# Spectral gate with a Mish layer: one program part per engine, or all instructions in the main block

## The chip, the cores and the metric

The kernel runs on one core of a Trainium2 chip. The metric is the device time of one execution in microseconds (us). Before the change it is 132.66 us, the median of three runs (132.80, 132.24, 132.66). A core has five engines, each with an instruction stream of its own: PE (matmul, with PEld for its weight loads), ACT, DVE, POOL and SP, which here only issues DMAs and waits. The streams meet only through semaphores: an instruction can wait until a semaphore has reached a value, and can add to one when it is done.

## The reference

```python
x = A_x                                            # 1 x 2048 x 512, bf16
g = sigmoid((x * gate_w).sum(-1, keepdims=True))   # one gate per row
X = rfft2(x.astype(float32), axes=(-2, -1))        # A: a filter in the spectrum
a = irfft2(X * (A_w_r + 1j * A_w_i), s=(2048, 512)).astype(bfloat16)
h = x @ B_w1 + B_b1                                # B: 512 -> 1792
act = h * tanh(softplus(h))                        #    Mish
b = act @ B_w2                                     #    1792 -> 512
return g * a + (1 - g) * b
```

## The kernel before

The 2048 rows are 16 tiles of 128. Branch B is two matmul stages on PE: the first (line 865) forms 14 blocks of 128 hidden columns for each of four chunks of 512 rows, with Mish on ACT (line 870) as it leaves PSUM; the second (line 883) sums 14 products for each row tile. Branch A is done as small matmuls with constant matrices: a transform over the columns (line 622), further ones (637, 716), the filter as DVE products in SBUF (735, 738, 742), and the way back (798, 837), whose results are mixed in by line 891 or by lines 906 and 910. Line 897 (ACT) and line 900 (DVE) scale the sums by 1 - g into the output buffer, which eight DMAs from SP and one from ACT write out (issued at line 485).

The program first gathers all of this as tasks in a graph (`_Graph.add`). `place` goes through a string, ORDER, that names each task in a fixed order, with its engine and its buffers; from it come one list of tasks per engine and the tasks each one waits for. `emit` (line 279) then gives out the instructions. Its inner function `run` (line 293) goes through the list of one engine: it emits the waits (`wait_ge`, line 299), the task's instructions, and the increments. For SP, `run` ends with waits for every DMA semaphore that SP has not waited for yet, the last being `out_sem`, which counts the nine output DMAs:

```python
            if ename == "sp":
                for t in self.tasks:
                    if t.isdma and t.sem is not out_sem:
                        wait(t.sem, t.semval)
                wait(out_sem, 16 * n_out)
```

`run` is called from five small functions inside `with nc.Block() as block:` (line 325). Such a block gives each engine a part of the program of its own. A part begins with a branch from the main block and ends with a branch to a common closing part, in which the five engines meet in a barrier: each one drains (waits until its own instructions are done), adds one to a gather semaphore (96) and waits for a release semaphore (97), which POOL raises when all the others have come. The five functions stand in the order PE, ACT, DVE, POOL, SP.

Ahead of the block, and not part of the change, the object that holds the program writes four small constants with POOL and makes the engines meet in a barrier of the same kind. These rows of the profile stand at line 953, where that object is made.

Of the kernel before, what the change touches and what calls it, by code (L numbers as in the profile page):

```python
# [186 lines left out]
class _Graph:  # L187
# [91 lines left out]
    def emit(self, nc, eng_sem, out_sem, n_out):  # L279
        order = self.order  # L280
        need = set()
        for t in self.tasks:
            for d in t.deps:
                if not d.isdma and not (d.eng == t.eng == "pe"):
                    need.add(id(d))
        for e in ("pe", "act", "dve", "pool"):
            n = 0
            for t in order[e]:
                if id(t) in need:
                    n += 1  # L290
                    t.sig = n

        def run(ename, eobj):
            seen = {}

            def wait(sem_, val):
                if seen.get(sem_.num, 0) < val:
                    seen[sem_.num] = val
                    eobj.wait_ge(sem_, val)

            for t in order[ename]:
                want = {}
                for d in t.deps:
                    if d.isdma:
                        sem_, val = d.sem, d.semval
                    elif d.eng == ename == "pe":
                        continue
                    else:
                        sem_, val = eng_sem[d.eng], d.sig
                    if want.get(sem_.num, (None, 0))[1] < val:  # L310
                        want[sem_.num] = (sem_, val)
                for sem_, val in want.values():
                    wait(sem_, val)
                ins = t.fn(eobj)
                if t.isdma:
                    ins.then_inc(t.sem, 16)
                elif t.sig:
                    ins.then_inc(eng_sem[ename], 1)
# [3 lines that stand above are left out]
                        wait(t.sem, t.semval)  # L322
                wait(out_sem, 16 * n_out)

        with nc.Block() as block:
            @block.tensor
            def _(e):
                run("pe", e)

            @block.scalar  # L330
            def _(e):
                run("act", e)

            @block.vector
            def _(e):
                run("dve", e)

            @block.gpsimd
            def _(e):
                run("pool", e)  # L340

            @block.sync
            def _(e):
                run("sp", e)


ORDER = """
# [620 lines left out]
```

## Time and profile before

| | before |
|---|---|
| median of 3 runs | 132.66 us (132.24 to 132.80) |
| the profiled execution: its own time | 132.7 us |
| its span, from the first to the last of the program's own instructions | 130.6 us |
| what lies around the span | 2.1 us |
| instructions in the trace | 2554 |
| PE busy | 123.9 us (95%) |
| PEld busy | 66.3 us (51%) |
| DVE busy | 92.9 us (71%) |
| ACT busy | 74.0 us (57%) |
| POOL busy | 4.7 us (4%) |
| granted TensorE clock, mean | 0.997 |
| instruction fetches, queue q8 | 8 packets, 0.13 MB |

How to read it: the span is cut by the program's own instructions. Barriers, waits, branches and DMA issues are instructions with rows, but do not count as busy. The trace also holds a record of every change of a semaphore with its time; this record goes on after the span, where the runtime closes the execution with instructions that have no rows here. In the profile, "q" behind an engine's name (SPq) means its sequencer, the part that fetches, waits and issues. L325 is line 325.

### The profile page before, as it was taken

The page shows a single profiled execution, that of the slowest core. Times are in us where ns is not written, and L with a number is a line of the kernel's source. Part 1 is how long each engine was busy: PE and PEld are TensorE (multiplying, and loading weights), DVE is VectorE, ACT ScalarE, POOL GpSimd, SP SyncE. Part 2 cuts the span into 40 slices and gives each one's busy share as a digit, 9 for nine tenths or more (in the row PEclk, how much of TensorE's full clock was granted, in tenths as well). Part 3 has the DMA queues.
Part 4 walks back from the last instruction along what each step waited for, and adds up shares of the span by engine and source line. Part 5 has one row for each costly group of instructions (what it writes and reads, how often), then busy time and mean ns, then how long its engine had stood idle before and what let it go on. Part 6 is the DMA issues. An engine that isn't in the chain of part 4 may idle for free.

```text
span 130.6 us, 2554 instructions
## 1 busy us (share of the span) xinstructions
PE 123.9 (95%) x1058; PEld 66.3 (51%) x1076; DVE 92.9 (71%) x161; ACT 74.0 (57%) x105; POOL 4.7 (4%) x8
## 2 busy tenths in 40 slices
PE   7989999999999999999999999999999999999990
PEld 4844566665654445444454445546654544444440
DVE  0773797999995899999999996237198692712820
ACT  3564989999999879998968024255431520001102
POOL 2000000000470000000000000000000000000000
PEclk9999999999999999999999999999999999999998
DMA  3889998878899989997400002020000002000671
GB/s 104 248 270 366 302 132 280 124 98 112 242 157 139 229 129 318 373 338 257 156 5 0 0 0 55 0 82 0 5 0 0 5 0 80 0 0 0 235 287 40
DMA packets 17302, 16.88 MB, mean 129 GB/s; under 512 B 7628, under 2 KB 14668, under 8 KB 17228
## 3 DMA queue, kind: packets, MB, share of 16 engines
q1 hardware_dynamic: 17120, 16.60, 52.8%
q8 instruction: 8, 0.13, 0.4%
q10 hardware_dynamic: 172, 0.13, 0.3%
q14 instruction: 2, 0.02, 0.1%
HBM read 13.05 MB, written 2.10 MB: 116 GB/s over the span
## 4 chain that ended last, share of the span: by engine, by line
PE 55%; DVE 28%; ACT 5%; DMA 5%; issue 2%; SPq 2%; DVEq 0%
PE ps L883 27%; PE ps L865 14%; DVE rE L742 8%; DVE tmp L735 6%; DMA w_sb<-in_B_w_dram 5%; DVE rC L738 4%; PE ps L837 3%; PE ps L798 3%; PE ps L637 3%; SPq L485 2%; ACT rC L522 2%; DVE rW L667 2%; PE ps L622 2%; DVE rW L679 2%; PE ps L891 1%
## 5 line engine op out<-in xcount | busy, mean ns | idle before, releaser
L865 PE MATMUL ps<-rX,w_sb 128*128 128x512 bf16 x215 | 49.5, 379 | 1.5 <-DMA w_sb<-in_B_w_dram 0.8
L865 PEld LDWEIGHTS ps<-rX,w_sb 128*128 128x128 bf16 x224 | 21.2, 98 | 24.3 <-DMA w_sb<-in_B_w_dram 1.3
L897 ACT ACTIVATE rX<-ps,omg 128x512 bf16<-128x512 f32 x10 | 6.9, 687 | 37.4 <-PE ps L891 22.6
L883 PE MATMUL ps<-w_sb,hs 128*128 128x512 bf16 x107 | 24.2, 379 | 0.6 <-issue 0.3
L870 ACT ACTIVATE hs<-ps,b1f 128x512 bf16<-128x512 f32 x28 | 18.2, 705 | 4.0 <-PE ps L865 2.8
L883 PEld LDWEIGHTS ps<-w_sb,hs 128*128 128x128 bf16 x112 | 10.5, 98 | 11.9
L883 PE MATMUL ps<-w_sb,rD 128*128 128x512 bf16 x54 | 12.5, 379 | 0.2 <-ACT tmp L844 0.2
L883 PE MATMUL ps<-w_sb,rS 128*128 128x512 bf16 x54 | 12.5, 379 | 0.1
L848 DVE TENSOR_TENSOR rA<-tmp,ps 128x512 bf16<-128x512 f32 x16 | 10.0, 680 | 3.4 <-PE ps L837 3.4
L735 DVE TENSOR_TENSOR tmp<-rC,rA 64x1024 bf16<-64x1024 bf16 x16 | 10.8, 685 | 1.9 <-ACT rC L522 1.5
L522 ACT ACTIVATE rC<-ps 128x1024 bf16<-128x1024 f32 x11 | 11.3, 1059 | 1.0 <-PE ps L716 0.6
L604 DVE TENSOR_TENSOR rB<-rA 128x256 bf16<-128x256 bf16 (+1 forms) x14 | 5.8, 458 | 6.5 <-DMA rA<-in_A_x_dram 6.5
L611 DVE SCALAR_TENSOR_TENSOR rA<-rA,tmp 128x512 bf16<-128x512 bf16 x16 | 10.0, 686 | 0.2
L742 DVE TENSOR_TENSOR rE<-rC,tmp 128x1024 bf16<-128x1024 bf16 x8 | 9.8, 1224 | 0.3
L870 ACT ACTIVATE rD<-ps,b1f 128x512 bf16<-128x512 f32 x14 | 9.0, 692 | 0.9 <-PE ps L865 0.9
L870 ACT ACTIVATE rS<-ps,b1f 128x512 bf16<-128x512 f32 x14 | 8.6, 689 | 1.4 <-PE ps L865 1.4
L910 DVE SCALAR_TENSOR_TENSOR rX<-ps,gcol,rX 128x512 bf16<-128x512 f32 x8 | 5.6, 745 | 5.1 <-PE ps L906 5.1
L883 PEld LDWEIGHTS ps<-w_sb,rS 128*128 128x128 bf16 x56 | 5.5, 98 | 6.6
L900 DVE TENSOR_SCALAR rX<-ps,omg 128x512 bf16<-128x512 f32 x6 | 4.5, 747 | 5.8 <-PE ps L891 4.0
L883 PEld LDWEIGHTS ps<-w_sb,rD 128*128 128x128 bf16 x56 | 5.3, 98 | 6.3
L519 DVE CAST rC<-ps 128x1024 bf16<-128x1024 f32 x5 | 6.0, 1223 | 2.0 <-PE ps L622 2.0
L522 ACT ACTIVATE rF<-ps 128x1024 bf16<-128x1024 f32 x5 | 4.9, 1021 | 3.8 <-PE ps L798 3.8
(77 smaller groups left out, 116.2 us busy)
## 6 DMA issues: line engine op xcount, KB each, us to landing
rF<-c_m SPq DMA_DIRECT2D x4, 512.0 KB, 7.5
rB<-c_g SPq DMA_DIRECT2D x4, 512.0 KB, 7.8
out_dram<-rX SPq DMA_DIRECT2D x7, 256.0 KB, 2.4
rA<-in_A_x_dram SPq DMA_DIRECT2D x3, 512.0 KB, 7.0
w_sb<-in_B_w_dram SPq DMA_DIRECT2D x2, 640.0 KB, 10.3
w_sb<-in_B_w_dram SPq DMA_DIRECT2D x2, 512.0 KB, 8.9
rS<-in_A_w_i_dram SPq DMA_DIRECT2D x3, 257.0 KB, 6.9
rS<-in_A_w_r_dram SPq DMA_DIRECT2D x3, 257.0 KB, 8.4
```

The lines of the kernel that those rows point to most:

```text
L519: return e.tensor_copy(out=o(), in_=i())
L522: return e.activation(o(), i(), AF.Copy)
L604: return e.tensor_tensor(out=xu[:, a:b_, uv, :], in0=x_sb[:, a:b_, 0:256], in1=x_sb[:, a:b_, 256:512], op=ALU.add if uv == 0 else ALU.subt ...
L611: t_gt.append(G.add(f"gt{t}", [("dve", 0.6, lambda e, t=t: e.scalar_tensor_tensor(out=x_sb[:, t, :], in0=x_sb[:, t, :], scalar=1.0, in1=tb ...
L735: return e.tensor_tensor(out=z3(z)[lo], in0=y3[hi], in1=wi3[hi], op=ALU.mult)
L742: return e.tensor_tensor(out=Yhq[:, q, h], in0=v(yv), in1=v(tb(z)), op=ALU.add)
L848: return e.tensor_tensor(out=yb[:, t:t + 2, 256 * h:256 * h + 256].rearrange("p t (i e) -> p t i e", e=2), in0=t4(z), in1=o4(bank(b, 1)), ...
L865: ins = e.matmul(bank(b), w1_sb[:, dt_, 128 * ft:128 * (ft + 1)], xT[:, c, dt_, :, :], start=(dt_ == 0), stop=(dt_ == 3))
L870: G.add(f"h{c}_{ft}", [("act", act(512, 1), lambda e, c=c, ft=ft, b=b: e.activation(hs[c][:, ft, :], bank(b), AF.Mish, bias=b1f[:, ft:ft + ...
L883: ins = e.matmul(bank(b)[:, 0:hi - lo], hs[c][:, ft, 128 * tl:128 * (tl + 1)], w2_sb[:, ft, lo:hi], start=(ft == 0), stop=(ft == NFT - 1 a ...
L897: return e.activation(bs[:, t, lo:hi], bank(b)[:, lo:hi], AF.Copy, scale=omg[:, t:t + 1])
L910: return e.scalar_tensor_tensor(out=bs[:, t, :], in0=bank(b), scalar=gcol[:, t:t + 1], in1=bs[:, t, :], op0=ALU.mult, op1=ALU.add)
```

## The change

The block and its five functions go; a loop calls `run` for each engine, SP first, while the main block is open. So the five lists stand one after the other in the main block, behind the barrier at its start. The branches to the parts and out of them and the barrier that closed the block are not made. Which instructions an engine gets from its list, their order on that engine, and the values they wait for come from the same lists as before. SP's waits at the end of `run` stay.

```diff
-        with nc.Block() as block:
-            @block.tensor
-            def _(e):
-                run("pe", e)
-
-            @block.scalar
-            def _(e):
-                run("act", e)
-
-            @block.vector
-            def _(e):
-                run("dve", e)
-
-            @block.gpsimd
-            def _(e):
-                run("pool", e)
-
-            @block.sync
-            def _(e):
-                run("sp", e)
+        for ename, eobj in (("sp", nc.sync), ("pe", nc.tensor), ("act", nc.scalar), ("dve", nc.vector), ("pool", nc.gpsimd)):
+            run(ename, eobj)
```

## The prediction

> **What bounds the kernel now.** I read the page first. PE is busy 95% of the span, and the chain that ended last is PE and DVE work; neither has anything to do with this edit.
>
> ```profile
> span 130.6 us, 2554 instructions
> ...
> PE 55%; DVE 28%; ACT 5%; DMA 5%; issue 2%; SPq 2%; DVEq 0%
> ```
>
> No arithmetic, no DMA and no wait of an engine's list is touched, so the change can only act where the parts are entered and where they are left. Next I read the end in the timeline.
>
> ```profile
> 127.14 0.38 PE L891 MATMUL ps<-rA,rC 128*128 128x512 bf16 x1
> 127.56 0.69 ACT L897 ACTIVATE rX<-ps,omg 128x512 bf16<-128x512 f32 x1 [6.44 <-PE ps L891]
> 128.28 0.39 ACTq L485 DMA_DIRECT2D out_dram<-rX  x1
> ```
>
> The last matmul ends at 127.5, ACT scales its result and issues the last output DMA by 128.66. The waits of SP's own queue say what comes behind it:
>
> ```profile
> SPq L299 <- DMA out_dram<-rX: 4.5, 1, 4.5
> ...
> SPq L325 <- PEq L325: 0.2, 1, 0.2
> ```
>
> SP sits 4.5 us for the output DMAs (L299), and the span ends only with the barrier, L325. All rows of L325:
>
> ```profile
> L325 POOLq EVENT_SEMAPHORE  x2: 17/17/17, 130.4 to 130.5; - x2
> L325 POOLq DRAIN  x1: 3997/3997/3997, 34.3 to 34.3; - x1
> L325 PEldq DRAIN  x1: 4075/4075/4075, 123.5 to 123.5; - x1
> L325 DVEq DRAIN  x1: 791/791/791, 124.3 to 124.3; - x1
> L325 ACTq DRAIN  x1: 143/143/143, 128.7 to 128.7; - x1
> L325 SPq COMPARE_BRANCH  x1: 33/33/33, 130.2 to 130.2; - x1
> L325 SPq DRAIN  x1: 13/13/13, 130.4 to 130.4; - x1
> L325 SPq EVENT_SEMAPHORE  x1: 17/17/17, 130.5 to 130.5; - x1
> L325 ACTq EVENT_SEMAPHORE  x1: 17/17/17, 130.5 to 130.5; - x1
> L325 DVEq EVENT_SEMAPHORE  x1: 21/21/21, 130.5 to 130.5; - x1
> L325 PEldq EVENT_SEMAPHORE  x1: 51/51/51, 130.5 to 130.5; - x1
> ```
>
> Columns: count, duration in ns, start of first and last. The reader is to see two things. Four engines came to the barrier long before the end: POOL's drain began at 34.3 and ended at 38.3, DVE's ended at 125.1, PE's at 127.57, ACT's at 128.84. The long drains (4075 ns on PE) lie beside matmuls that run anyway; only SP is late, at 130.4. And of the ten branches that a block implies, one alone has a row, SP's at the end, which carries a wait.
>
> The end in nanoseconds, from the instruction and semaphore records: the output semaphore gets its last increment at 130.113; SP's wait row for it stands at 130.130 to 130.157; the branch at 130.200 to 130.233; SP's drain at 130.367 to 130.380; POOL's two rows from 130.405 to 130.500; the last row, PE's, ends at 130.588. Behind the span the record of semaphore 2 goes on. Its changes, in us:
>
> ```
> after the last row:     130.857 130.891 131.068 131.112 131.135 | 131.233 131.271 131.306 131.353
> after the sem resets:   132.141 132.175 132.213 132.258 132.281 | 132.379 132.418 132.452 132.498
> ```
>
> That is a barrier of the runtime's, a chain through five engines and back. [...] The same chain runs just ahead of the span, ends at 0.001, and the first own instruction behind it is SP's (0.000, 0.231 behind the fifth step), the last PE's (0.316). I read from both that the chain goes PE first and SP last (fifth step), and back.
>
> **The change, term by term** (against the profiled execution: 132.7, span 130.588, rest 2.11; the median 132.66 is 0.04 below it).
>
> *Entry.* The barrier at line 953 stays. No entry branch has a row. PE's first weight load starts 25 ns after its release row ends (0.773 to 0.798); in mid-kernel, behind the wait row that ends at 4.820, it is 25 ns as well. SP's first DMA issue starts 62 ns after its release row, against 30 to 47 ns behind its wait rows at 46.917, 58.406 and 121.165. So entry is worth between 0 and 0.03; I take 0, by PE's row. [...]
>
> *The middle.* Each engine's list, its order and its waits stay: 0. What hides an unequal arrival of the engines at entry is the entry barrier, which stays.
>
> *SP's tail.* Its seven remaining waits lie on three wait rows of two and on the branch, which waits for the DMA of the bias. Without the branch the seventh needs a row of its own or a place on another. Bounds: nothing (SP is done at 130.157), or one more row by the nearest pair, 43 ns of gap and 17 ns: 130.217. I take the second, since the rows hold two waits each.
>
> *The closing barrier.* Twelve rows go (five drains, six semaphore rows, one branch); none but SP's and POOL's last ones are on the path. The span then ends with SP's last row: 130.588 - 130.217 = **0.37 less**; 0.43 if the wait is packed.
>
> *The runtime's chain.* What is late next? In before, all five engines leave the block's barrier together at 130.50 to 130.59, and SP's step of the chain comes at 131.135, because the four steps ahead of it need from 130.857 to 131.112. After the change those four engines are at the chain early: ACT, the last of them, is through at 128.66. Their steps are then made while SP still waits for the DMA, and only SP's own way to the chain remains. It has no row. [...] From above POOL's way, 0.57 (130.500 to 131.068; the step before it took 0.034, this one 0.177, so POOL was late). I take **0.20**, near the 0.231 that SP needed at the start. Then SP's step comes at 130.217 + 0.20 = 130.42 instead of 131.135: **0.72 less in all**, of which 0.37 is in the span and 0.35 behind it. Everything behind that step is a fixed chain and moves with it.
>
> [...] The trace has 0.75 us from the span's end to the ninth step.
>
> **Sum:** 132.7 - 0.72 = 131.98 for the profiled execution; against the median 132.66 - 0.72 = **131.94 us**, 0.54% less. A measurement of this kernel can tell about 0.5% from no change (0.66 us; the three runs spread over 0.56), so the forecast lies at that edge.
>
> **The rivals.**
>
> *Only the span shrinks.* SP's way to the runtime's chain is as long as POOL's (0.57) or the early engines don't make their steps ahead. For it: that way has no row, and POOL's was long. Against it: PE's took 0.269. The time: 132.66 - 0.37 = 132.29, or 132.31 with POOL's 0.57 (130.217 + 0.57 = 130.79 against 131.135). Chance 0.2.
>
> *It doesn't do what it says.* The main block is closed by a barrier of its own, as it is opened by one (L953, which no line of the kernel asks for). Then the drains come back under another line: 132.66. Against it: the rows of before show no second closing barrier behind L325. Chance 0.1.
>
> *Slower: instruction fetch.* All streams now stand in one block. Were an engine's stream fetched worse, PE would pay: q8 holds 8 packets in 0.4% of 16 engines' 130.6 us, 0.004 x 16 x 130.6 / 8 = 1.04 us each. One fetch laid bare turns -0.72 into +0.32, two into +1.36, 134.0; over the bound from the second on. For it: only that the layout changes. Against it: idle time put to "issue" comes to at most 0.3 at a line on PE, and behind the entry to at most 1.3 on PEld (L837, in three pieces, none over 0.4), so these fetches are hidden, and an engine's stream is as long as before. Chance 0.07.
>
> *More.* Packed wait, shorter way of SP (0.13), entry 0.03: 0.06 + 0.07 + 0.03 more, 131.78, or 131.5 with the runs' spread. Chance 0.05.
>
> **How the numbers follow.** The forecast has 0.58 and by itself the range 131.7 to 132.2 (its bounds 131.8 to 132.0, with some of the runs' spread). The range that should hold 8 in 10 takes in the first rival and half of the second: 131.55 to 132.7; left out are slower (0.07), the upper half of "no change" (0.05) and a low tail (0.04). Faster by over 0.5% means below 132.0: six tenths of the forecast (0.35), "more" (0.05) and chance hits of the first rival (0.03), 0.43. Slower 0.07. The rest, 0.50, lies within.
>
> **What would show it.** Right: no rows of line 325's kind at the end, 2543 instructions (12 fewer, one wait more), the span's last row a wait of SP within 0.1 us of the last output increment, span 130.2, and 1.7 to 1.85 us around it. The first four steps of semaphore 2 would stand ahead of SP's last row, before 129.2. First rival: these steps behind 130.2, and 2.1 us or more around the span. Second: five drains. Third: PE gaps under "issue" near 1 us. Wrong in any case if an engine's order or waits in mid-kernel differ.

## The result and the profile after

The changed kernel takes 131.70 us against 132.67 us, medians of 22 runs each. The ratio is 0.9931, 95% interval 0.9912 to 0.995: 0.92 us less, by the interval 0.66 to 1.17 (the two medians by themselves lie 0.97 apart). The profiled execution took 131.67 us with a span of 130.1.

The first and the chain line of the page after; 18 lines of the program went, so line 883 is 865 now, 865 is 847, 485 is 467:

```profile
span 130.1 us, 2561 instructions
...
PE 56%; DVE 28%; ACT 5%; DMA 5%; SPq 2%; issue 2%; DVEq 0%
```

The chain is the one of before. The instruction count seems to have grown from 2554; but before's page has 1058 matmul records and this one all 1076. Without those 18 it is 2543: twelve rows fewer and one wait more.

The end, in the timeline of after (start, duration, what):

```profile
127.08 0.38 PE L873 MATMUL ps<-rA,rC 128*128 128x512 bf16 x1
127.50 0.69 ACT L879 ACTIVATE rX<-ps,omg 128x512 bf16<-128x512 f32 x1 [6.43 <-PE ps L873]
128.22 0.38 ACTq L467 DMA_DIRECT2D out_dram<-rX  x1
```

It is before's end, 0.06 earlier. The waits of SP's queue, and the rows of line 299, in after:

```profile
SPq L299 <- DMA out_dram<-rX: 4.5, 1, 4.5
```

```profile
L299 SPq EVENT_SEMAPHORE  x10: 17/17/28, 47.2 to 130.1; - x10
```

SP still sits 4.5 us for the output DMAs. Its last wait row, at 130.1, is now the last row of the program: the L325 rows have no successor under any line. It is the tenth such row (nine before), but the added one lies at 125.4, ahead of the long wait. The seventh wait, the bias's, which had been on the branch, shares the last row with the output semaphore.

A single execution's middle differs from the next one's by more than this change is worth (the 22 spans of after run from 129.0 to 130.8). So I read the end from the last increment of the output semaphore on. In the semaphore record of after (us):

```
last output increment    130.047
SP's last row            130.063 to 130.091
semaphore 2, there       127.639 128.863 128.902 128.946 130.236
semaphore 2, and back    130.280 130.318 130.353 130.401
the chain behind it      131.193 ... 131.550
```

No row of the program names semaphore 2, in before or after (they name 96, 97 and 99 to 140). From that I take its steps to be the runtime's; which engine makes which is read from the runs further on. "Resets" are single changes of semaphores 7 to 255 behind the span, in before from 131.265 to 131.917, in after from 130.370 to 130.968; whose they are and to what value, these records don't show.

Before, all nine of the first chain's steps stood behind the span's last row. Now four stand ahead of SP's last row, and only SP's own step waits for the DMA. From the last output increment it is 0.189 to SP's step and 1.503 to the last step of all, against 1.022 and 2.385 before: 0.882 less. What lies around the span fell from 2.11 to 1.58 in the profiled executions; by the medians it is 1.54 now, against 1.95 in the 33 runs of before that were made beside the first experiments.

Such a reading is one execution's. Two kernels further on that should end as this one does (SP's list last, early loads) reach the last step 1.515 and 1.524 behind the increment, so differences of 0.02 to 0.03 mean nothing here. The early steps take no semaphore away from an engine that still works: in all ten traces the first of the resets comes 0.130 to 0.140 behind SP's step, when the last engine has come, and in after only semaphores 2, 100 and 103 change between the first early step and SP's.

### The profile page after: what moved, and what is told of

Its sections match the earlier page's. It is cut to its first block, busy times and chain, and to the rows that moved or that the text cites. A ratio compares the mean times of both kernels' runs of the same rounds, so it can differ in the third digit from the quotient of the medians.

```text
span 130.1 us, 2561 instructions
## 1 busy us (share of the span) xinstructions
PE 124.7 (96%) x1076; PEld 65.2 (50%) x1076; DVE 92.8 (71%) x161; ACT 74.0 (57%) x105; POOL 4.7 (4%) x8
## 4 chain that ended last, share of the span: by engine, by line
PE 56%; DVE 28%; ACT 5%; DMA 5%; SPq 2%; issue 2%; DVEq 0%
PE ps L865 28%; PE ps L847 14%; DVE rE L724 8%; DVE tmp L717 6%; DMA w_sb<-in_B_w_dram 5%; DVE rC L720 4%; PE ps L819 3%; PE ps L780 3%; PE ps L619 3%; SPq L467 2%; ACT rC L504 2%; DVE rW L649 2%; PE ps L604 2%; DVE rW L661 2%; PE ps L873 1%
## 5 line engine op out<-in xcount | busy, mean ns | idle before, releaser
L847 PE MATMUL ps<-rX,w_sb 128*128 128x512 bf16 x224 | 50.8, 379 | 1.5 <-DMA w_sb<-in_B_w_dram 1.5
L865 PE MATMUL ps<-w_sb,hs 128*128 128x512 bf16 x112 | 25.2, 379 | 0.0
```

Source lines behind the costliest of these rows:

```text
L847: ins = e.matmul(bank(b), w1_sb[:, dt_, 128 * ft:128 * (ft + 1)], xT[:, c, dt_, :, :], start=(dt_ == 0), stop=(dt_ == 3))
L865: ins = e.matmul(bank(b)[:, 0:hi - lo], hs[c][:, ft, 128 * tl:128 * (tl + 1)], w2_sb[:, ft, lo:hi], start=(ft == 0), stop=(ft == NFT - 1 a ...
```

## The experiments

My theory had three parts: SP's branch, the rows of the closing barrier, and the runtime's chain, which the early engines can now enter ahead. The main rival was the layout: one block, five lists in it, no branches at entry. All kernels below compute the whole reference.

**The barrier put back, without the parts.**

```diff
             run(ename, eobj)
+        nc.all_engine_barrier()
```

> The changed kernel (one main block) with one all-engine barrier put behind the loop: the closing barrier without the parts and without SP's branch. Theory (the gain is the closing barrier, SP's branch, and the steps of the runtime's chain that the early engines now make ahead): nearly all of it goes back. SP's drain comes about 45 ns behind its last wait row instead of 210, so 0.17 us of the branch stays won: about 132.5, ratio to before 0.9987; around the span 2.1 again; the five steps of semaphore 2 all behind the last row. Rival (the gain comes from the layout, one block instead of parts, or from the entry): it stays at 131.7, ratio 0.993.

Measured: ratio 0.9988 (0.996 to 1.0016), 132.27 us. The rows of the barrier's line in this kernel (count, ns, first and last start):

```profile
L327 POOLq EVENT_SEMAPHORE  x2: 17/17/17, 130.3 to 130.4; - x2
L327 POOLq DRAIN  x1: 3996/3996/3996, 34.4 to 34.4; - x1
...
L327 SPq DRAIN  x1: 7/7/7, 130.3 to 130.3; - x1
L327 SPq EVENT_SEMAPHORE  x1: 17/17/17, 130.5 to 130.5; - x1
...
L327 PEldq EVENT_SEMAPHORE  x1: 51/51/51, 130.5 to 130.5; - x1
```

The rows are those of L325 before, without the branch. SP's wait row ends at 130.263 and its drain starts at 130.303, 0.040 later, where before it was 0.210. From the last increment to the last step of all it is 2.208, 0.177 less than before. Around the span it is 1.98 (median), back from 1.54. So nearly all of the gain goes with the barrier, although the instructions stand in one block.

**The parts kept, without the barrier.** This is the kernel before; the closing part's instructions are taken out.

```diff
             def _(e):
                 run("sp", e)
+
+        end = [b for b in nc.main_func.blocks if b.name == block.end_bb][0]
+        end.instructions = []
```

> The kernel before, its five parts and branches kept, with the instructions of the closing barrier taken out of the closing part. Theory: nearly the whole gain is there; SP's branch row (33 ns and the 134 ns behind it) stays and costs about 0.17: 131.9, ratio 0.994; the first four steps of semaphore 2 stand ahead of SP's last wait; around the span 1.6 to 1.7. Rival (layout or entry): 132.7, ratio 1.0.

Measured: ratio 0.9936 (0.9909 to 0.9964), 131.87 us, 1.59 around the span. One row of the block's line is left:

```profile
L325 SPq COMPARE_BRANCH  x1: 33/33/33, 129.7 to 129.7; - x1
```

Four steps of semaphore 2 stand at 127.239 to 128.546, ahead of SP's wait row at 129.665. To the last step it is 1.657, 0.154 more than in the changed kernel. The four kernels make a square:

| from the last output increment to the last step, us | with barrier | without |
|---|---|---|
| parts and branch | 2.385 (before) | 1.657 |
| one block | 2.208 | 1.503 (after) |

The barrier is worth 0.705 to 0.728, whichever goes first. The branch and the layout change together in the other direction, 0.154 to 0.177; that this is the branch's is read from where it lies. Without the barrier SP's last wait row ends 0.044 behind the increment in both layouts, and with the branch SP's step comes 0.345 behind it instead of 0.189. The other engines show nothing of it: ACT's early step comes 0.261 behind the end of its last row with the parts and without. So nothing is left for the layout at the end of the program. SP's branch is also the only one with a row, and it carries a wait; whether the branch or the wait on it costs the time, these runs don't separate. This branch has a row of 33 ns and costs 0.15 to 0.18 us on the path.

**Every engine waits for the outputs.** No barrier and no branch, but no engine is early:

```diff
             run(ename, eobj)
+        for eobj in (nc.tensor, nc.scalar, nc.vector, nc.gpsimd):
+            eobj.wait_ge(out_sem, 16 * n_out)
```

> The changed kernel, in which PE, ACT, DVE and POOL also wait for the output DMAs at their end, as SP does; no barrier, no branch. Theory (part of the gain is that four engines make their steps of the runtime's chain early): the span grows by under 0.1, but the chain starts only behind the last output DMA: SP's step comes 0.2 (PE's way of 0.27 and four steps) to 0.55 (POOL's way as long as in before) later, 131.9 to 132.25, ratio 0.994 to 0.997; around the span 1.8 to 2.1. Rival (only the removed rows count): 131.7 to 131.8, around the span 1.6.

Measured: ratio 0.9988 (0.9966 to 1.0009), 132.62 us, 2.02 around the span. The added rows:

```profile
L328 ACTq EVENT_SEMAPHORE  x1: 17/17/17, 131.0 to 131.0; - x1
L328 POOLq EVENT_SEMAPHORE  x1: 17/17/17, 131.0 to 131.0; - x1
L328 DVEq EVENT_SEMAPHORE  x1: 21/21/21, 131.0 to 131.0; - x1
L328 PEldq EVENT_SEMAPHORE  x1: 51/51/51, 131.0 to 131.0; - x1
```

The span ends 0.080 behind the last increment, against 0.044 in the changed kernel: these rows cost next to nothing in it. Yet the last step comes 2.000 behind the increment, 0.497 later than in the changed kernel. The steps of semaphore 2 say why: 131.220, 131.254, then 131.523, 131.567, 131.590. The third, POOL's, is 0.269 behind the second, where it is 0.039 in after. POOL's wait row had ended at 130.991, 0.532 before its step. The rival that only the removed rows count falls. By the ratio it lost more than I had expected, but the interval reaches the expected 0.997; the median of 132.62 even lies 0.10 above that of before's runs beside it (132.52), a difference that the intervals don't support.

**One engine at a time waits for the outputs**, with a line such as this (PE; in the other two `nc.gpsimd` or `nc.vector`):

```diff
             run(ename, eobj)
+        nc.tensor.wait_ge(out_sem, 16 * n_out)
```

PE: 

> The changed kernel, in which PE alone also waits for the output DMAs at its end. Theory (the chain goes PE, ACT, POOL, DVE, SP): with its first engine late all five steps come behind the last output DMA, PE's about 0.2 to 0.3 after it and SP's 0.14 later: 0.2 to 0.3 over the changed kernel, 131.9 to 132.0, ratio 0.994 to 0.995; the spacing of the five steps is regular (35, 38, 44, 23 ns), since POOL is ready. Rival (PE is not first, or early steps don't matter): no change from 131.7.

POOL: 

> The changed kernel, in which POOL alone also waits for the output DMAs at its end. Theory (POOL's own way to the runtime's chain is the longest, 0.53 from its wait row to its step in the run where all engines wait): POOL's step stands 0.55 behind the last output increment, DVE's and SP's 0.04 and 0.07 later: 0.45 over the changed kernel, 132.15, ratio to before 0.997. Rival (POOL was late there only because it is the third of the chain): its step stands as PE's did, 0.25 to 0.3 behind the increment: 131.85, ratio 0.9945.

DVE: 

> The changed kernel, in which DVE alone also waits for the output DMAs. Theory (DVE is the last but one of the chain and its way is as short as SP's): its step about 0.2 behind the last increment and SP's 0.02 later; DVE's second step 0.1 behind instead of 0.04: 0.05 to 0.1 over the changed kernel, 131.8, ratio 0.9935 to 0.994. Rival (any engine that comes late costs as much as PE did, 0.26): 131.95, ratio 0.995.

The added rows, one from each kernel in this order:

```profile
L327 PEldq EVENT_SEMAPHORE  x1: 51/51/51, 129.8 to 129.8; - x1
```

```profile
L327 POOLq EVENT_SEMAPHORE  x1: 17/17/17, 129.9 to 129.9; - x1
```

```profile
L327 DVEq EVENT_SEMAPHORE  x1: 21/21/21, 130.2 to 130.2; - x1
```

| who waits beside SP | steps of semaphore 2 up to SP's, from the last increment | last step | ratio to before |
|---|---|---|---|
| nobody (after) | PE, ACT, POOL, DVE early; SP 0.189 | 1.503 | 0.9931 (0.9912 to 0.995) |
| DVE | three early; DVE 0.194, SP 0.218 | 1.611 | 0.9947 (0.9907 to 0.9987) |
| PE | 0.271, 0.305, 0.344, 0.388, 0.411 | 1.766 | 0.9965 (0.9946 to 0.9984) |
| POOL | two early; POOL 0.574, DVE 0.617, SP 0.640 | 2.006 | 0.9973 (0.9932 to 1.0013) |
| all | 0.271, 0.305, 0.574, 0.618, 0.641 | 2.000 | 0.9988 (0.9966 to 1.0009) |

The order of the chain is as the prediction read it: whichever of the three waits, the steps ahead of its own place are early and those behind it follow. (ACT was not made to wait; that it is second is read from after, where the second step, at 128.863, comes 0.261 behind ACT's last row.) PE late pulls all five behind the increment, and they come evenly, 34, 39, 44 and 23 ns apart. POOL late costs as much as all four late: POOL's way from its wait row to its step, 0.533, is what everyone had waited for. Why it is so long, no run shows. DVE late costs little at SP's step (0.029) and 0.08 more behind it. Of this, 0.05 is DVE's second step, which comes 0.120 behind its own first one (130.409 and 130.529), and 0.096 behind SP's instead of the 0.044 of after, where DVE's first stood 1.290 ahead of SP's. In before, where it stood 0.023 ahead, the second came 0.098 behind SP's. The other 0.03 lies behind the ninth step, where the resets end 0.595 behind it instead of 0.567; the kernel with SP's list last, in which DVE doesn't wait, has 0.593 there, so it is scatter. The rivals of POOL and DVE fall: POOL's step is 0.574 behind the increment, not 0.25 to 0.3, and DVE late costs 0.11, not 0.26. POOL's own cost, 0.503, is 0.05 over the expected 0.45, about what DVE's second step differs by (0.098 behind SP's in before, 0.044 in after).

The ratios, whose intervals are 0.4 to 0.8% wide, keep this order, but alone could not tell neighbours apart; the nanoseconds of the record do (but for POOL and all, 0.006 apart), each from one execution. PE's expected ratio, 0.994 to 0.995, was too low by 0.0015, within its interval; by the record it lost 0.263, as expected.

**SP's list last in the loop.**

```diff
-        for ename, eobj in (("sp", nc.sync), ("pe", nc.tensor), ("act", nc.scalar), ("dve", nc.vector), ("pool", nc.gpsimd)):
+        for ename, eobj in (("pe", nc.tensor), ("act", nc.scalar), ("dve", nc.vector), ("pool", nc.gpsimd), ("sp", nc.sync)):
```

> The changed kernel with the loop in the order PE, ACT, DVE, POOL, SP, so that SP's list stands last in the main block. Theory (the place in the block has no effect, each engine has its own stream): 131.7, ratio 0.993, and the same times from the last output increment on. Rival (a part of the gain comes from SP's list standing first): up to 0.3 slower, ratio 0.995.

Measured: 131.69 us, ratio 0.9949 (0.9913 to 0.9985); 1.515 to the last step, 0.178 to SP's. The median is that of the changed kernel (131.70) and the end is the same to 0.012. The interval of the ratio holds both theories' values, so the ratio alone doesn't decide; the end does, for no effect.

**The same idea at the start.** The barrier at line 935 (953 before) holds SP until 0.73, though its loads need nothing that the barrier guards.

```diff
             run(ename, eobj)
+        bb = nc.cur_bb.bb
+        ins = list(bb.instructions)
+        sp = [i for i in ins if i.engine == mybir.EngineType.SP]
+        i0 = next(k for k, i in enumerate(sp) if isinstance(i, mybir.InstDMACopy))
+        rel = sp[i0 - 1]
+        ins.remove(rel)
+        ins.insert(ins.index(sp[i0 + 9]) + 1, rel)
+        bb.instructions = ins
```

> The changed kernel, in which SP's release row of the barrier at the start (line 935) is moved behind SP's first ten DMA issues; SP's own step of that barrier stays where it was. A use of the same idea at the other end: the loads need nothing that the barrier guards. Theory: SP's first issue comes at about 0.05 instead of 0.79, and the chain at the start (SP's issues, then the load of w_sb that PE waits for until 10.1) moves with it, so the whole run comes 0.5 to 0.75 earlier: 131.0 to 131.2, ratio 0.988 to 0.990. Rival (at the start the DMA engines or PE's own work set the time): 131.7, ratio 0.993.

Measured: 130.86 us, ratio 0.9897 (0.9849 to 0.9944). The chain at the start, first of the changed kernel, then of this one (start, duration, what):

```profile
0.73 0.06 issue
0.79 0.39 SPq L467
...
4.11 5.89 DMA w_sb<-in_B_w_dram
10.00 0.05 issue
10.05 1.04 PE ps L847 x4
```

```profile
0.01 0.08 issue
0.09 0.40 SPq L476
...
3.42 5.71 DMA w_sb<-in_B_w_dram
9.12 0.05 issue
9.17 1.90 PE ps L856 x8
```

The whole chain moved by 0.70 at SP's first issue and by 0.88 at PE, since the load that PE waits for also took 0.18 less in this execution. The median is 0.83 below that of the kernel with SP last, run on the same chip, and a little below the expected 131.0 to 131.2. By the ratios it is 1.03% below before, about 1.4 us, and 0.5%, about 0.7 us, below the kernel with SP last. It has the lowest median here. That it beats the changed kernel itself rests on medians of different sessions (131.70) and on the kernel with SP last; the intervals of the ratios overlap, so the times alone don't settle it. The shift of 0.70 at SP's first issue is the firm part.

## Why the prediction was right, and where its sizes were off

- **What is touched.** Right: the chain of the middle is unchanged, and the last output increment stands where it stood. By the median span and the 0.044 behind the increment it is at 130.1 in the changed kernel (130.15 - 0.04), and at 130.1 in before (130.6 - 0.475, with the 33 runs beside the first experiments).
- **Entry, taken as 0.** Right: the first rows behind the starting barrier are the same to 3 ns (SP's issue at 0.789 and 0.790, PE's first load at 0.798 and 0.797).
- **SP's tail.** The seventh wait was taken as a row of its own (0.06); it costs nothing, the lower of the two bounds. The span's end moved by 0.43, not 0.37.
- **What is late next.** Right, and the main step: SP's own way to the chain, with the other engines through before 129.2 (the last early step is at 128.946). With PE alone late the gain shrinks by 0.263, with POOL alone late by 0.503: the early steps matter, as the prediction said.
- **The size of SP's way.** Taken as 0.20, under POOL's 0.57 and PE's 0.269 (130.588 to 130.857); it is 0.145 (130.091 to 130.236). The 0.13 in *More* is the time in before from the fifth step to the first of the resets (131.135 to 131.265); that this reset is SP's, no run shows, and what the runs showed in its place is the 0.145.
- **The way back of the chain.** Taken as fixed. It is not quite: DVE's second step came 0.098 behind SP's in before, where DVE had made its first 0.023 ahead of SP's, and 0.044 in after, where it had made it 1.290 ahead. A term of 0.05 that the prediction didn't have.
- **The sum.** 0.72 was forecast. With 0.06, 0.055 and 0.05 it is 0.885, against 0.882 in the record and 0.92 (0.66 to 1.17) in the times. The three are small, all on one side, and together put 131.70 below 131.94. It is the lower end of the range that the forecast had by itself (131.7 to 132.2), and the weak end of the measured interval, 0.995, still lies on the 0.5% edge.
- **Around the span.** 1.7 to 1.85 was named as the sign; it is 1.58. The last two of these terms make 0.10 of the difference to the 1.76 that the sum gives (2.11 - 0.35); the other 0.08 lies outside the semaphore record, and its cause is open.
- **The rivals.** *Only the span shrinks* fell: it needs SP's way to be like POOL's, 0.53 to 0.57. But POOL's length was real, and is what the runtime's chain had waited for in before: of the 0.882, 0.177 is the branch (before to barrier put back), 0.208 the barrier's rows (that kernel to all waiting) and 0.497 the early steps (all waiting to after), set by POOL's way: POOL alone late costs as much, and PE alone late 0.263. *More* came nearest, although it had a chance of 0.05 only: two of its three terms came in nearly whole, the wait that shares a row (0.06) and SP's shorter way (0.055 of 0.07), while the third, the entry, gave nothing and the way back was not in it. That these went the same way is in part luck; but the prediction had named both smaller values (the wait on another row, and the 0.13) and took neither. *It doesn't do what it says* fell: no closing barrier came under another line. *Instruction fetch*: q8 holds 8 packets as before, and the idle time put to "issue" on PE shows no new gap: the largest, on PEld, is 1.3 in three pieces of up to 0.4 in both.
- **What the chain costs.** That depends on who is late: from the last output increment to the ninth step it took 1.240 us in before and 0.354 in after. (From the span's end to the ninth step of before it is 0.77, not the 0.75 of the prediction: 130.588 to 131.353.) From the first step to the ninth, the chain ahead of before's span took 0.372, and the one of the run where PE waits 0.357 (130.083 to 130.440), so the traces agree.

## What to carry to other kernels

When a program ends with a barrier and the runtime meets the engines again behind it, look whether the first barrier does more than keep the early engines from doing their closing work early; in this kernel it did not. Then let each engine run off its end, and let one engine hold the wait for the output DMAs: one with a short way from its last row to the runtime's chain and the last place in it, here SP (0.145 us), and by these runs not POOL (0.53). All of this was seen in one kernel on one core. Look at both ends of the span, and read such small terms from the last event that all versions share, not from times whose spread is as large.

## What the runs showed of the hardware

- POOL needed 0.53 us from its last row to its step of the runtime's chain (0.532 and 0.533), PE 0.19 (129.892 to 130.083; with the closing barrier 0.27 in before and 0.24 where it was put back), SP and DVE 0.15 (0.145 and 0.146). In before and in the run with the barrier put back POOL's way was 0.57 (0.568 and 0.567), and it set the end: its step came 0.177 and 0.207 behind the one ahead of it.
- SP's closing branch, which carries a wait and has a row of 33 ns, cost 0.15 to 0.18 us. The nine others of the block left no row; where they could be timed (the entry, to 3 ns, and ACT's end, 0.261 with and without) they cost nothing.
- The steps of the chain behind the span lay 23 to 48 ns apart in before and after, but for those that waited for a late engine (POOL's 0.177 in before, ACT's and SP's in after) and DVE's second: that came 0.096 to 0.098 behind SP's where DVE had made its first 0.023 or 0.024 ahead of SP's (before, and DVE waiting), and 0.044 where it had made it 1.290 ahead (after).
- The barrier at the start kept SP's first load back by 0.70 us (0.79 to 0.09), and moving one row of it was worth 0.7 us by the ratios and 0.83 by the medians, nearly as much as the whole change.
